# 33-point Fourier stage: a second buffer for a chunk's fp16 pair, and a chunk's loading, folding and splitting queued one unit of work sooner

## The chip, the cores and the metric

One core of a Trainium2 chip runs the whole kernel in one launch. The metric is device time in microseconds (us): the median of three runs for the kernel before, and each change is judged by its time beside it. Engines are called as in the profile: PE (TensorE, matmuls; PEld its weight loads), DVE (VectorE), ACT (ScalarE), POOL (GpSimd), SP (SyncE, which issues most DMAs).

## The reference

The input x is 4 batches of 4224 tokens with 192 features. Three layers follow each other; the change lies in the third.

```python
def _moe2_ref(x, w_ch1, w_ch2):
    X = np.fft.fft(x, axis=1)
    X = np.fft.fft(X, axis=2)
    mixed = np.real(X).astype(np.float32)
    u = x + mixed
    mu = np.mean(u, axis=-1, keepdims=True)
    var = np.mean((u - mu) ** 2, axis=-1, keepdims=True)
    un = (u - mu) / np.sqrt(var + 1e-06)
    ch = np.maximum(un @ w_ch1, 0.0) @ w_ch2
    return (u + ch).astype(np.float32)
```

The layers ahead of it are a causal softmax convolution of 7 taps, and a token mixing of rank 32 with a feed-forward net of the same shape (192 to 768 to 192, ReLU between).

## The kernel before

**Blocks.** The two feed-forward nets are the bulk of the work. 4 batches x 11 blocks of 384 tokens x 2 nets make 88 blocks, in the order net 1 of batch 0, 1, 2, then net 2 of batch 0, net 1 of batch 3, then net 2 of batch 1, 2, 3. Matmuls are made of fp16 pairs (a high part and a remainder), three or so matmuls for one. `layer1` (L623 to L629) makes two of six hidden tiles at a time: PE writes a PSUM tile, ACT takes the ReLU and its high part (`hh`, L628), DVE the remainder (`hl`, L629). `layer2` (L648 to L655) of the block before makes one of three output tiles. All PSUM tiles come from one pool of 8 buffers, and most of them are given back by a DVE instruction.

**Slots.** The program is written out by hand in slots, three to a block (r = 0, 1, 2). A slot issues two units of `layer1`, then parts of the preparation of a later block, one unit of `layer2`, and last, in `fill`, units of other work. In net 2 the preparation (`pre2`) takes statistics on DVE in slot 0 (L568 to L572), a root on ACT and the scale and shift on DVE in slot 1 (L583 to L591), and in slot 2 the normalised rows on ACT (L597, L600) and their fp16 remainder (L604, on POOL or DVE), which SP transposes into `ch`. Each engine runs its instructions in the order in which they are written here.

**The Fourier transform.** `fft_units(b)` cuts the transform of batch b in units. `fill` spreads them evenly over a window of slots (slot 0 is the first of the program): slots 37 to 69 for batch 0, 98 to 126 for batch 1, 150 to 176 for batch 2 and 190 to 214 for batch 3, so a batch has 33, 29, 27 and 25 slots for the same 17 units of its first half. The first half is the 33-point stage over 22 groups of rows, in 6 chunks of 4 (the last has 2). For one chunk c:

- `loadx(c)`: three DMAs on SP bring rows into `x33` (one buffer), and up to four gathers on POOL (L707, one each group) bring the mirrored rows into `xm` (two buffers). The first half of the gathers is called G0 here, the second G1 (the last chunk has a single gather and no G1).
- `fold(c)`: three DVE instructions (L741, L742, L744) and one of POOL (L746) add and subtract the two.
- `split33(c)`: ACT scales `xm` (L753) and writes its high part into the pair `xp` (L754), POOL its remainder (L755). `xp` has one buffer.
- `s33(c, 0)` and `s33(c, 1)`: 12 matmuls each on the pair (L774), then ACT (L781) and DVE (L782) write the result z and give the PSUM tile back.

In the list of units, the unit called a(c) holds `s33(c, 0)` and the unit m(c) holds `s33(c, 1)`. Ahead of its matmuls a(c) has `fold(c + 1)` and behind them G0 of chunk c + 2; m(c) has `split33(c + 1)` ahead and G1 of chunk c + 2 behind. Five units stand ahead of a(0); a(c) is unit 5 + 2c of 17 counted from 0, m(c) unit 6 + 2c. In batch 3 this puts every a(c) in a slot r = 2 and every m(c) in a slot r = 0, so a(c) to m(c) is one slot and m(c) to a(c + 1) two. In batch 2 the same holds from m(0) to a(3); in batches 0 and 1 the units fall on changing slots.

Of the kernel before, what the change touches and what calls it, by code (L numbers as in the profile page):

```python
# [7 lines left out]
F16 = mybir.dt.float16  # L8
# [8 lines left out]
B, S, D = 4, 4224, 192  # L17
# [18 lines left out]
XG = 4  # L36
# [59 lines left out]
def build(tc, io):  # L96
# [4 lines left out]
    def pool(name, bufs, **kw):  # L101
        return ctx.enter_context(tc.tile_pool(name=name, bufs=bufs, **kw))

    cst = pool("cst", 1)
    wrk = pool("wrk", 2)
# [10 lines left out]
    def all_max(out, x):  # L116

        ps = psm("am")
        nc.tensor.matmul(ps[:, :P], lhsT=x.broadcast_to([P, P]), rhs=sel[:, 1], start=True, stop=True)
        nc.vector.tensor_reduce(out=out, in_=ps[:, :P], axis=AX.X, op=ALU.max)  # L120

    def run(units):
        for f in units:
            if f is not None:
                f()

    with tc.manual_schedule():
# [548 lines left out]
        def fft_units(b):  # L676
# [6 lines left out]
            def scale():  # L683

                m = xmax[b]
                nc.vector.tensor_reduce(out=m[:, 11:12], in_=m[:, 0:NB], axis=AX.X, op=ALU.max)

            def scale2():
                m = xmax[b]
                all_max(m[:, 12:13], m[:, 11:12])  # L690
                nc.vector.tensor_scalar(out=m[:, 12:13], in0=m[:, 12:13], scalar1=1e-30,
                                        scalar2=2.0 ** -13, op0=ALU.max, op1=ALU.mult)
                nc.vector.reciprocal(m[:, 13:14], m[:, 12:13])
                nc.vector.tensor_scalar(out=m[:, 14:15], in0=m[:, 12:13], scalar1=2.0 ** 11,
                                        scalar2=None, op0=ALU.mult)
                st["s"], st["r"] = m[:, 13:14], m[:, 14:15]

            def loadx(c, part=None):

                g0, ng = chunks[c]  # L700
                nn = min(ng, GT - g0)
                if part != 1:
                    xs[c] = load_rows(g0, ng, nn)
                half = (nn + 1) // 2
                for g in range(nn) if part is None else (range(half), range(half, nn))[part]:
                    k = 16 + g0 + g
                    nc.gpsimd.indirect_dma_start(  # L707
                        out=xs[c][1][:, g], out_offset=None, in_=x2d[b][:],
                        in_offset=bass.IndirectOffsetOnAxis(ap=mrow[:99, k:k + 1], axis=0))

            def load_rows(g0, ng, nn):
                x = wrk.tile([99, XG, D], F32, name="x33", bufs=1)
                y = wrk.tile([99, XG, D], F32, name="xm", bufs=2)
                src = x2d[b]
                if nn < ng:
                    nc.gpsimd.memset(x[64:99, nn], 0.0)
                    nc.gpsimd.memset(y[:, nn], 0.0)
                    for i in range(2):
                        nc.sync.dma_start(
                            x[33 * i:33 * i + 33, nn],  # L720
                            bass.AP(tensor=src.tensor, offset=src.offset + 33 * 64 * i * D,
                                    ap=[[P * D, 33], [1, D]]))
                for i in range(3):
                    nc.sync.dma_start(
                        x[33 * i:33 * i + 33, :nn],
                        bass.AP(tensor=src.tensor,
                                offset=src.offset + (33 + 99 * g0 + 33 * i) * D,
                                ap=[[P * D, 33], [99 * D, nn], [1, D]]))
                return x, y

            def fold(c):

                ng = chunks[c][1]
                x, y = [t[:, :ng] for t in xs[c]]
                l, r = slice(1, 96), slice(96, 191)
                v = y[:, :, r]
                a = list(list(w) for w in v.ap)
                swap = bass.AP(tensor=v.tensor, offset=v.offset,
                               ap=[a[0], [D, ng], [-95, 2], [1, 95]])
                m = x[:, :, 1:191].rearrange("p g (h n) -> p g h n", h=2)  # L740
                nc.vector.tensor_tensor(out=m, in0=m, in1=swap, op=ALU.add)  # L741
                nc.vector.tensor_tensor(out=y[:, :, 0:97:96], in0=x[:, :, 0:192:191],  # L742
                                        in1=y[:, :, 0:192:191], op=ALU.add)
                nc.vector.tensor_tensor(out=y[:, :, l], in0=x[:, :, l], in1=x[:, :, r],  # L744
                                        op=ALU.add)
                nc.gpsimd.tensor_tensor(out=y[:, :, 97:192], in0=x[:, :, l], in1=x[:, :, r],  # L746
                                        op=ALU.subtract)

            def split33(c):
                n = chunks[c][1] * D  # L750
                x = xs[c][1].rearrange("p g d -> p (g d)")[:, :n]
                t = wrk.tile([99, 2, XG * D], F16, name="xp", bufs=1)
                nc.scalar.activation(x, x, AF.Identity, scale=st["s"][:99])  # L753
                nc.scalar.activation(t[:, 0, :n], x, AF.Identity)  # L754
                nc.gpsimd.tensor_tensor(out=t[:, 1, :n], in0=x, in1=t[:, 0, :n], op=ALU.subtract)  # L755
                xs[c] = t

            def s33(c, e):

                if "z" not in st:  # L760
                    st["z"] = z_tile().rearrange("p (e l k n) -> p e l k n", e=2, l=2, k=17)
                g0, ng = chunks[c]
                m, c0 = ((KD, 0), (D - KD, KD))[e]
                x = xs[c]
                nn = min(ng, GT - g0)
                ps = psm("s33")
                for g in range(ng):
                    if g < nn:
                        w, kr, o = tabs["w33"], 99, ps[:m, 102 * g:102 * g + 102]
                    else:  # L770
                        w, kr, o = tabs["w33s"][:, e], 66, ps[:m, 102 * g:102 * g + 34]
                    cols = slice(g * D + c0, g * D + c0 + m)
                    for n, (xq, wq) in enumerate(((0, 0), (0, 1), (1, 0))):
                        nc.tensor.matmul(o, lhsT=x[:kr, xq, cols], rhs=w[:kr, wq],  # L774
                                         start=(n == 0), stop=(n == 2))
                for a, n, o in ((1 + 3 * g0, 3 * nn, 0), (0, ng - nn, 102 * nn)):
                    if n:
                        v = ps[:m, o:o + 34 * n].rearrange("p (n k) -> p k n", k=34)
                        hi, lo = [st["z"][:m, e, l].rearrange("p k (f n) -> p (k f) n", f=2)
                                  [:, :, a:a + n] for l in range(2)]  # L780
                        nc.scalar.activation(hi, v, AF.Identity, scale=2.0 ** -11)  # L781
                        nc.vector.scalar_tensor_tensor(out=lo, in0=v, scalar=2.0 ** -11, in1=hi,  # L782
                                                       op0=ALU.mult, op1=ALU.subtract)
# [80 lines left out]
                nc.gpsimd.tensor_tensor(out=y1, in0=y1, in1=near(1, 1), op=ALU.add)  # L864

            last = len(chunks) - 1
            first = [lambda: (scale(), loadx(0)), scale2, lambda: (fold(0), loadx(1)), lambda: split33(0), None]
            for c in range(len(chunks)):
                a, m = [lambda c=c: s33(c, 0)], [lambda c=c: s33(c, 1)]
                if c < last:  # L870
                    a.insert(0, lambda c=c: fold(c + 1))
                    m.insert(0, lambda c=c: split33(c + 1))
                if c + 1 < last:
                    a.append(lambda c=c: loadx(c + 2, 0))
                    m.append(lambda c=c: loadx(c + 2, 1))
                first += [lambda a=a: run(a), lambda m=m: run(m)]
            todo = [8] + list(range(8))
            out = [lambda: (loadu(8), loadu(0)), lambda: sd(8)]
            for i, j in enumerate(todo):
                a, m = [lambda j=j: s128(j)], [lambda j=j: adds(j)]  # L880
# [106 lines left out]
        play(0)  # L987

        ft = [fft_units(b) for b in range(B)]

        windows = [[28, 32, [load_tables]],
# [16 lines left out]
        last, pre = None, [(None, None)] * 4  # L1008
        for i in range(nblk + 1):
# [15 lines left out]
            last = layer2(*blocks[i]) if i < nblk else None  # L1025
# [57 lines left out]
```

## Time and profile before

| | |
|---|---|
| median of 3 runs | 1019.2 us (1017.62 to 1020.02) |
| the profiled execution | 1028.63 us, span 1026.8 us |
| granted TensorE clock, mean | 0.997 |
| busy: PE / DVE / ACT / POOL | 989.8 / 764.0 / 605.2 / 373.9 us |
| share of the span: PE / DVE / ACT / POOL | 96% / 74% / 59% / 36% |

The profiled execution is one run of the program, and it took 9.4 us longer than the median. The span is from its first to its last instruction. Idle time of an engine is put down to what ended it: "<-POOL xp L755" is the wait that the POOL instruction of line 755 ended. A clock of 1.00 is TensorE's 2.4 GHz, 0.50 its 1.2 GHz.

### The profile page before, as it was taken

The page shows a single profiled execution, that of the slowest core. Times are in us where ns is not written, and L with a number is a line of the kernel's source. Part 1 is how long each engine was busy: PE and PEld are TensorE (multiplying, and loading weights), DVE is VectorE, ACT ScalarE, POOL GpSimd, SP SyncE. Part 2 cuts the span into 40 slices and gives each one's busy share as a digit, 9 for nine tenths or more (in the row PEclk, how much of TensorE's full clock was granted, in tenths as well). Part 3 has the DMA queues.
Part 4 walks back from the last instruction along what each step waited for, and adds up shares of the span by engine and source line. Part 5 has one row for each costly group of instructions (what it writes and reads, how often), then busy time and mean ns, then how long its engine had stood idle before and what let it go on. Part 6 is the DMA issues. An engine that isn't in the chain of part 4 may idle for free.

```text
span 1026.8 us, 25594 instructions
## 1 busy us (share of the span) xinstructions
PE 989.8 (96%) x9929; PEld 776.4 (76%) x9929; DVE 764.0 (74%) x2092; ACT 605.2 (59%) x1482; POOL 373.9 (36%) x367
## 2 busy tenths in 40 slices
PE   8789999999999999999999999999999999999998
PEld 5466777777777877777778877777887777787777
DVE  7766776788876666877777777897887687687674
ACT  2555557666766666656656666656556565555552
POOL 0001001344632333346534435663255751562100
PEclk9999999999999999999999999999999999999999
DMA  8597757665646665444344455332544342433221
GB/s 286 162 227 251 208 135 200 194 168 135 168 105 179 187 180 143 94 107 112 96 127 112 138 136 148 101 88 64 119 112 93 106 86 64 131 101 71 59 59 58
DMA packets 179283, 136.32 MB, mean 133 GB/s; under 512 B 116666, under 2 KB 152737, under 8 KB 178393
## 3 DMA queue, kind: packets, MB, share of 16 engines
q1 hardware_dynamic: 171575, 121.64, 44.5%
q0 software_dynamic: 7104, 12.70, 4.6%
q8 instruction: 77, 1.26, 0.5%
q14 instruction: 45, 0.37, 0.1%
q10 hardware_dynamic: 482, 0.35, 0.1%
HBM read 61.69 MB, written 46.11 MB: 105 GB/s over the span
## 4 chain that ended last, share of the span: by engine, by line
PE 56%; DVE 7%; issue 4%; POOL 4%; DMA 3%; ACT 0%; DVEq 0%; POOLq 0%; ACTq 0%
PE l L652 8%; PE l L648 8%; PE l L650 8%; PE l L623 5%; PE l L627 5%; PE l L624 5%; PE l L626 5%; PE l L625 5%; POOL xm L707 2%; DVE hl L629 2%; PE sd L814 2%; DMA xm<-x2d,mrow 2%; DMA ch<-sp 2%; PE s L830 2%; DVE x L741 1%
## 5 line engine op out<-in xcount | busy, mean ns | idle before, releaser
L648 PE MATMUL l<-w2h,hh 128*128 128x192 f16 x1584 | 391.0, 247 | 1.9 <-DVE u L655 0.9
L650 PE MATMUL l<-w2l,hh 128*128 128x192 f16 x1584 | 390.8, 247 | 1.5 <-DVE w2l L262 1.2
L652 PE MATMUL l<-w2h,hl 128*128 128x192 f16 x1584 | 390.8, 247 | 1.4 <-DVE hl L629 0.9
L628 ACT ACTIVATE hh<-l 128x384 f16<-128x384 f32 x528 | 249.7, 488 | 224.8 <-PE l L627 209.4
L629 DVE SCALAR_TENSOR_TENSOR hl<-l,hh 128x384 f16<-128x384 f32 x528 | 278.7, 551 | 80.4 <-ACT hh L628 72.1
L623 PE MATMUL l<-ch,w1h 128*128 128x384 f16 x528 | 172.9, 327 | 15.2 <-DMA ch<-sp 8.8
L624 PE MATMUL l<-ch,w1l 128*128 128x384 f16 x528 | 172.0, 326 | 0.7 <-issue 0.7
L627 PE MATMUL l<-ch,w1h 128*128 128x384 f16 x528 | 172.5, 327 | 0.0
L626 PE MATMUL l<-ch,w1l 128*128 128x384 f16 x528 | 172.4, 327 | 0.0
L625 PE MATMUL l<-ch,w1h 128*128 128x384 f16 x528 | 172.1, 326 | 0.0
L648 PEld LDWEIGHTS <-hh 128*128 128x128 f16 x1584 | 155.5, 98 | 19.3 <-issue 3.2
L650 PEld LDWEIGHTS <-hh 128*128 128x128 f16 x1584 | 155.5, 98 | 17.9 <-issue 2.3
L548 POOL TENSOR_TENSOR sp<-un,sp 128x576 f16<-128x576 f32 x44 | 57.3, 1301 | 300.5 <-ACT sp L544 252.5
L652 PEld LDWEIGHTS <-hl 128*128 128x128 f16 x1584 | 155.5, 98 | 4.3 <-issue 2.5
L604 POOL TENSOR_TENSOR sp<-un,sp 128x576 f16<-128x576 f32 x34 | 45.5, 1339 | 158.5 <-ACT sp L600 150.7
L707 POOL DMA_INDIRECT xm<-x2d,mrow x84 | 84.4, 1005 | 21.2 <-issue 18.0
L655 DVE SCALAR_TENSOR_TENSOR u<-l,cmax,u 128x192 f32<-128x192 f32 x132 | 54.8, 416 | 41.5 <-PE l L652 25.6
L655 DVE SCALAR_TENSOR_TENSOR u<-l,ws,u 128x192 f32<-128x192 f32 x132 | 54.4, 412 | 36.4 <-PE l L652 26.9
L623 PEld LDWEIGHTS <-w1h 128*128 128x128 f16 x528 | 51.6, 98 | 35.5 <-DMA ch<-sp 10.8
L625 PEld LDWEIGHTS <-w1h 128*128 128x128 f16 x528 | 51.5, 97 | 34.9 <-issue 0.7
L627 PEld LDWEIGHTS <-w1h 128*128 128x128 f16 x528 | 51.6, 98 | 34.3 <-issue 0.2
L626 PEld LDWEIGHTS <-w1l 128*128 128x128 f16 x528 | 51.5, 98 | 34.4 <-issue 0.2
(138 smaller groups left out, 1414.7 us busy)
## 6 DMA issues: line engine op xcount, KB each, us to landing
x2d<-u SPq DMA_DIRECT2D x68, 288.0 KB
u<-x1d SPq DMA_DIRECT2D x44, 288.0 KB
out_d<-u SPq DMA_DIRECT2D x43, 288.0 KB
x1d<-xw SPq DMA_DIRECT2D x36, 210.0 KB
u<-x2d SPq DMA_DIRECT2D x32, 192.0 KB
x<-x2d SPq DMA_DIRECT2D x60, 99.0 KB
xw<-x_d SPq DMA_DIRECT2D x4, 1344.0 KB
xw<-x_d SPq DMA_DIRECT2D x8, 672.0 KB
```

Source lines behind the costliest of these rows:

```text
L623: nc.tensor.matmul(o, lhsT=w["h1"][:, 0, ms], rhs=kd[0], start=True, stop=False)
L624: nc.tensor.matmul(o, lhsT=w["l1"][:, 0, ms], rhs=kd[0], start=False, stop=False)
L625: nc.tensor.matmul(o, lhsT=w["h1"][:, 1, ms], rhs=kd[1], start=False, stop=False)
L626: nc.tensor.matmul(o, lhsT=w["l1"][:, 1, ms], rhs=kd[1], start=False, stop=False)
L627: nc.tensor.matmul(o, lhsT=w["h1"][:, 2, ms], rhs=kd[2], start=False, stop=True)
L628: nc.scalar.activation(hh[:, m], ps[:, :TB * P], AF.Relu)
L629: nc.vector.scalar_tensor_tensor(out=hl[:, m], in0=ps[:, :TB * P], scalar=0.0, in1=hh[:, m], op0=ALU.max, op1=ALU.subtract)
L648: nc.tensor.matmul(o, lhsT=hh[:, m, rs], rhs=w["h2"][:, m], start=(m == 0), stop=False)
L650: nc.tensor.matmul(o, lhsT=hh[:, m, rs], rhs=w["l2"][:, m], start=False, stop=False)
L652: nc.tensor.matmul(o, lhsT=hl[:, m, rs], rhs=w["h2"][:, m], start=False, stop=(m == NM - 1))
L655: nc.vector.scalar_tensor_tensor(out=u[:, r], in0=o, scalar=sc, in1=u[:, r], op0=ALU.mult, op1=ALU.add)
L707: nc.gpsimd.indirect_dma_start(out=xs[c][1][:, g], out_offset=None, in_=x2d[b][:], in_offset=bass.IndirectOffsetOnAxis(ap=mrow[:99, k:k + ...
```

## The change

`xp` gets two buffers. `loadx` of the first chunks is cut into its halves, and every step of a chunk's preparation stands one unit sooner: a(c) now has `split33(c + 1)` ahead of its matmuls and G1 of chunk c + 2 behind them; m(c) has `fold(c + 2)` ahead and G0 of chunk c + 3, with its three SP loads, behind. The five units ahead of a(0) take up what moved. Lines up to L866 keep their numbers, later ones move by up to four.

```diff
-                t = wrk.tile([99, 2, XG * D], F16, name="xp", bufs=1)
+                t = wrk.tile([99, 2, XG * D], F16, name="xp", bufs=2)
...
-            first = [lambda: (scale(), loadx(0)), scale2, lambda: (fold(0), loadx(1)), lambda: split33(0), None]
+
+            first = [lambda: (scale(), loadx(0, 0)), lambda: (scale2(), loadx(0, 1)),
+                     lambda: (fold(0), loadx(1, 0)), lambda: (split33(0), loadx(1, 1)),
+                     lambda: (fold(1), loadx(2, 0))]
             for c in range(len(chunks)):
                 a, m = [lambda c=c: s33(c, 0)], [lambda c=c: s33(c, 1)]
                 if c < last:
-                    a.insert(0, lambda c=c: fold(c + 1))
-                    m.insert(0, lambda c=c: split33(c + 1))
+                    a.insert(0, lambda c=c: split33(c + 1))
                 if c + 1 < last:
-                    a.append(lambda c=c: loadx(c + 2, 0))
-                    m.append(lambda c=c: loadx(c + 2, 1))
+                    a.append(lambda c=c: loadx(c + 2, 1))
+                    m.insert(0, lambda c=c: fold(c + 2))
+                if c + 2 < last:
+                    m.append(lambda c=c: loadx(c + 3, 0))
```

The order of PE's instructions stays the same, all 17593 of them. On the other engines the steps move past their neighbours. Three places in batch 3 show it; numbers behind a name are those of a buffer or a tensor and differ between the two programs.

DVE, before: scale and shift of a block in slot 1 (L583 to L591), `layer1` and `layer2` of slot 2, then a fold at its end, and the z of `s33(c, 0)`.

```order
L583 RECIPROCAL rs<-sd 128x3
L584 TENSOR_TENSOR sd<-rs 128x3
L585 SCALAR_TENSOR_TENSOR sd<-sd,va 128x3
L587 SCALAR_TENSOR_TENSOR rs<-sd,rs 128x3
L591 SCALAR_TENSOR_TENSOR mr<-mv,rs 128x3
L629 SCALAR_TENSOR_TENSOR hl<-l_12733,hh 128x384
L629 SCALAR_TENSOR_TENSOR hl<-l_12741,hh 128x384
L655 SCALAR_TENSOR_TENSOR u_11258<-l_12755,ws_3647,u_11258 128x192
L741 TENSOR_TENSOR x_12612<-x_12612,xm 99x4x190
L742 TENSOR_TENSOR xm<-x_12612,xm 99x8
L744 TENSOR_TENSOR xm<-x_12612 99x4x95
L782 SCALAR_TENSOR_TENSOR z<-s_12783,z 97x34x12
```

DVE, now: the fold stands at the end of slot 0, and the scale and shift of slot 1 come behind it.

```order
L741 TENSOR_TENSOR x_12506<-x_12506,xm 99x4x190
L742 TENSOR_TENSOR xm<-x_12506,xm 99x8
L744 TENSOR_TENSOR xm<-x_12506 99x4x95
L782 SCALAR_TENSOR_TENSOR z<-s_12677,z 95x34x12
L629 SCALAR_TENSOR_TENSOR hl<-l_12699,hh 128x384
L629 SCALAR_TENSOR_TENSOR hl<-l_12707,hh 128x384
L655 SCALAR_TENSOR_TENSOR u_11258<-l_12717,ws_3658,u_11258 128x192
L583 RECIPROCAL rs<-sd 128x3
L584 TENSOR_TENSOR sd<-rs 128x3
L585 SCALAR_TENSOR_TENSOR sd<-sd,va 128x3
L587 SCALAR_TENSOR_TENSOR rs<-sd,rs 128x3
L591 SCALAR_TENSOR_TENSOR mr<-mv,rs 128x3
```

The fold moved from the end of slot 2 to the end of slot 0, ahead of the five instructions that make `mr` and `rs`.

ACT, before: the normalised rows of slot 2 (L597, L600), the z of `s33(c, 0)`, two ReLUs of the next slot, and then the split (L753, L754).

```order
L597 ACTIVATE un<-u_11258,mr,rs 128x192 x3
L600 ACTIVATE sp<-un 128x3x192
L781 ACTIVATE z<-s_12597 97x34x12
L628 ACTIVATE hh<-l_12621 128x384
L628 ACTIVATE hh<-l_12629 128x384
L753 ACTIVATE xm<-xm,xmax 99x768
L754 ACTIVATE xp<-xm 99x768
L781 ACTIVATE z<-s_12671 95x34x12
```

ACT, now: the split stands in slot 2, right behind the normalised rows.

```order
L597 ACTIVATE un<-u_11258,mr,rs 128x192 x3
L600 ACTIVATE sp<-un 128x3x192
L753 ACTIVATE xm<-xm,xmax 99x768
L754 ACTIVATE xp<-xm 99x768
L781 ACTIVATE z<-s_12608 97x34x12
L628 ACTIVATE hh<-l_12627 128x384
L628 ACTIVATE hh<-l_12635 128x384
L781 ACTIVATE z<-s_12677 95x34x12
```

L753 and L754 moved ahead of one z and two ReLUs, and wait with the instructions that need `mr` and `rs`.

POOL, before: from one split (L755) to the next, with G1, a block's remainder (L604), the fold's POOL part and G0 between.

```order
L755 TENSOR_TENSOR xp<-xm,xp 99x768
L707 DMA xm<-x2d_73,mrow 99x192 x2
L604 TENSOR_TENSOR sp<-un,sp 128x3x192
L746 TENSOR_TENSOR xm<-x_12426 99x4x95
L707 DMA xm<-x2d_73,mrow 99x192 x2
L755 TENSOR_TENSOR xp<-xm,xp 99x768
```

POOL, now:

```order
L755 TENSOR_TENSOR xp<-xm,xp 99x768
L707 DMA xm<-x2d_73,mrow 99x192 x2
L746 TENSOR_TENSOR xm<-x_12314 99x4x95
L707 DMA xm<-x2d_73,mrow 99x192 x2
L604 TENSOR_TENSOR sp<-un,sp 128x3x192
L755 TENSOR_TENSOR xp<-xm,xp 99x768
```

The cycle of split, G1, fold and G0 is the same; L604 moved from ahead of the fold to ahead of the next split.

## Rows read from the trace of the kernel before

**Rows 1.** Page, part 1: busy time, share of the span, instructions.

```profile
PE 989.8 (96%) x9929; PEld 776.4 (76%) x9929; DVE 764.0 (74%) x2092; ACT 605.2 (59%) x1482; POOL 373.9 (36%) x367
```

**Rows 2.** Waits of PE: who was waited for, us in total, times, longest.

```profile
PE s L774 <- POOL xp L755: 5.8, 6, 1.4
PE s L774 <- ACT xp L754: 1.2, 1, 1.2
```

**Rows 3.** Timeline of PE, batches 1 and 2: start, duration, what, [idle before, its end].

```profile
486.47 0.34 PE L623 MATMUL l<-ch,w1h 128*128 128x384 f16 x1 [0.57 <-DVE hl L629]
497.66 0.67 PE L774 MATMUL s<-vt,xp 99*97 99x102 f16 x10 [0.76 <-POOL xp L755]
511.92 0.26 PE L652 MATMUL l<-w2h,hl 128*128 128x192 f16 x1 [0.93 <-DVE hl L629]
...
681.13 0.67 PE L774 MATMUL s<-vt,xp 99*97 99x102 f16 x10 [1.16 <-POOL xp L755]
693.27 0.29 PE L774 MATMUL s<-vt,xp 99*97 99x102 f16 x2 [1.17 <-ACT xp L754]
694.99 0.67 PE L774 MATMUL s<-vt,xp 99*97 99x102 f16 x10 [1.43 <-POOL xp L755]
```

**Rows 4.** Stretches of 1 us, PE alone: length, busy, granted clock, DMA share, GB/s.

```profile
696.00:697.00 1.00, 1.00 (x5) 0.52 0.53 202
...
699.00:700.00 1.00, 1.00 (x12) 0.78 1.07 204
```

**Rows 5.** Timeline of PE, batch 3.

```profile
793.25 0.72 PE L774 MATMUL s<-vt,xp 99*97 99x102 f16 x12
...
803.69 0.72 PE L774 MATMUL s<-vt,xp 99*97 99x102 f16 x12
...
811.74 0.32 PE L623 MATMUL l<-ch,w1h 128*128 128x384 f16 x1 [0.55 <-DVE z L782]
...
819.88 0.71 PE L774 MATMUL s<-vt,xp 99*95 99x102 f16 x12
...
827.81 0.67 PE L774 MATMUL s<-vt,xp 99*97 99x102 f16 x10 [0.90 <-POOL xp L755]
...
838.90 0.67 PE L774 MATMUL s<-vt,xp 99*97 99x102 f16 x10 [0.45 <-POOL xp L755]
```

**Rows 6.** Timelines of POOL, DVE and ACT, batch 3: one round, split to split.

```profile
809.56 0.95 DVE L741 TENSOR_TENSOR x<-x,xm 99x760 f32<-99x760 f32 x1 [4.50 <-issue]
814.55 1.65 POOL L755 TENSOR_TENSOR xp<-xm,xp 99x768 f16<-99x768 f32 x1
...
817.70 1.00 POOL L707 DMA_INDIRECT xm<-x2d,mrow  x1 [0.30 <-issue]
...
821.11 0.95 DVE L741 TENSOR_TENSOR x<-x,xm 99x760 f32<-99x760 f32 x1 [2.69 <-DMA xm<-x2d,mrow]
822.35 1.24 POOL L746 TENSOR_TENSOR xm<-x 99x380 f32<-99x380 f32 x1 [1.65 <-DVE xm L742]
823.62 0.94 ACT L753 ACTIVATE xm<-xm,xmax 99x768 f32<-99x768 f32 x1 [3.12 <-POOL xm L746]
...
826.10 1.65 POOL L755 TENSOR_TENSOR xp<-xm,xp 99x768 f16<-99x768 f32 x1
```

**Rows 7.** Timelines of DVE and ACT, batch 3, first chunk: fold to split.

```profile
780.23 0.94 DVE L741 TENSOR_TENSOR x<-x,xm 99x760 f32<-99x760 f32 x1
...
784.00 1.42 ACT L597 ACTIVATE un<-u,mr,rs 128x192 f32<-128x192 f32 x3 [1.39 <-DVE rs L587]
...
786.04 0.92 ACT L753 ACTIVATE xm<-xm,xmax 99x768 f32<-99x768 f32 x1
787.00 0.84 ACT L754 ACTIVATE xp<-xm 99x768 f16<-99x768 f32 x1
```

**Rows 8.** Timeline of DVE, batch 1: folds of chunks 3 and 4.

```profile
488.35 1.83 DVE L741 TENSOR_TENSOR x<-x,xm 99x760 f32<-99x760 f32 x1 [1.11 <-DMA xm<-x2d,mrow]
502.17 0.95 DVE L741 TENSOR_TENSOR x<-x,xm 99x760 f32<-99x760 f32 x1 [3.29 <-DMA xm<-x2d,mrow]
```

## The prediction

> **What bounds the kernel now.** The page comes first: PE is busy for 989.8 of 1026.8 us, so 37 us are idle at all [rows 1], and a change off PE can give back no more than its share of them. The waits of PE say which share is this stage's: the matmuls of `s33` waited 7.0 us in seven places for the pair, 5.8 for its remainder on POOL and 1.2 for its high part on ACT [rows 2]. The timeline of PE says where: none in batch 0, 0.76 in batch 1, 1.16 + 1.17 + 1.43 in batch 2 [rows 3], and 1.16 + 0.90 + 0.45 in batch 3, of which two rows stand in [rows 5]. Behind two of them in batch 2 the granted clock drops to 1.2 GHz for a while: 0.52 at 696 us, 0.50 in the two stretches between, 0.78 at 699 [rows 4], which costs 0.48 + 0.50 + 0.50 + 0.22 = 1.7 us of PE's work.
>
> Why is the pair late? In batch 3 PE needs 803.69 - 793.25 = 10.44 us for a chunk where nothing stops it [rows 5]. The pair's own preparation takes longer. It is a round through three engines, and since POOL works in order, each chunk starts where the last one ended: split on POOL (L755) 814.55, 1.65 long; then G1, whose second gather ends at 818.70; its data land and DVE folds at 821.11, 2.41 later; POOL's part 822.35 to 823.59; ACT's L753 at 823.62 (it had waited 3.12); next split at 826.10 [rows 6]. That is 11.55 us, 1.1 more than PE's 10.44, and the waits of batch 3 are what is left of it once the head start is used up. The one buffer of the pair is not in this round.
>
> **The change, part by part.**
>
> *Second buffer.* It frees ACT's L754 from waiting for `s33(c, 1)` and removes no instruction. PE gains by it only where the split comes sooner too.
>
> *Split one unit sooner.* `s33(c + 1, 0)` now stands two units behind its split. All seven waits should go, and the drop of the clock with them: 0.76 in batch 1, 3.76 + 1.7 in batch 2, the rest in batch 3.
>
> *Fold one unit sooner.* Here is the cost. G1 and the fold that needs it were m(c) and a(c + 1), two slots apart in batch 3; they are now a(c) and m(c), one slot apart. And the fold now stands at the end of slot 0, ahead of the five DVE instructions that make `mr` and `rs`; ACT's normalised rows wait for these, and the split stands behind those rows. So the round gets another member: fold, `layer1`, `layer2` and scale and shift of the next slot on DVE, normalised rows and split on ACT, split on POOL, G1, landing, next fold. Before, the fold stood behind the scale and shift, and ACT went from the fold's POOL part straight to the split.
>
> The new round can be measured, since the first chunk of batch 3 has this order already: its fold starts at 780.23, ACT's rows at 784.00 (having waited 1.39 for DVE's `rs`), L753 at 786.04, L754 ends at 787.84 [rows 7]. That is 7.6 us. With 1.65 for the split, 2.5 to the end of G1 and 2.4 to the landing [rows 6], the round is 14.2 us. The upper end is 14.9: other chunks have a z (L782) between, and the POOL gap may add a little. The lower end is the 11.55 of before. I take 14.2, since it consists of the very instructions. A second witness: in batch 1, where fold and split were already two slots apart, two folds stand 502.17 - 488.35 = 13.8 us apart, and DVE waited 3.29 for the gathers [rows 8].
>
> The Trainium skill ("DMA: Bandwidth & Descriptors", Anatomy of one DMA) gives a gather issued from POOL a fixed 2.0 us and its bytes at 436 GB/s, about 2.2 us for 76 KB as an estimate. From the gather's issue to the fold the rows show 3.4 (1.00 and 2.41), so the trace disagrees; by the page each round would be 1.2 us shorter and the whole sum about +3 in place of +10.
>
> What does a late fold do to PE? PE can run ahead until the eight PSUM tiles are used up. Behind the last `s33` ahead of a fold there are six tiles of two slots and one more `s33`; the next needs the z that DVE writes behind the fold. The rows show this limit once: the fold of 809.56 held z, and PE waited at 811.74, 2.18 later; the `s33` ahead had ended at 804.41, and the 6.78 us of work between were done at 811.19, where the wait of 0.55 began [rows 5, 6]. So a fold may start 6.78 - 2.18 = 4.6 us behind the end of the `s33` in its unit; what is beyond that, PE waits.
>
> Batch 3: with only G0 of chunk 1 ahead of it, the first split starts as L754 ends, 787.9, and ends at 789.5; G1 to 792.0, landing and fold of chunk 1 at 794.4. Three rounds of 14.2 on, the fold of chunk 4 starts at 837.0. Its unit m(2) cannot end before 837.0 - 4.6 = 832.4; it ended at 819.88 + 0.71 = 820.6 [rows 5]. That is +11.8, less the 0.90 and 0.45 that came later and go: **+10.5**. Bounds by the two rounds: +2.5 (11.55) and +12.5 (14.9). Chunk 5 has no G1 and ends the chain.
>
> Batch 2: two such rounds (chunks 2 to 4) against 10.44 each lose 7.5; a fold that is on time stands 1.4 to 4 us behind its `s33`, so some of the 4.6 is left. I take 6.5 lost (between 2.9, all of it left, and 7.5), less 3.76 + 1.7 gained: **+1.0** (-2.6 to +2.0).
>
> Batch 1: G1 and folds move from one or two slots apart to two, and splits to one or two: rounds get shorter. The 0.76 goes, and the 0.57 and 0.93 that PE waited for DVE's `hl` behind late folds [rows 3]: **-2.3** (bounds 0 and -2.3).
>
> Batch 0: its units are two slots apart before and after, and PE never waited for a pair. 0, within 1.
>
> Clock: new waits of 14.2 - 10.44 = 3.8 us, five of them, may each bring the 1.7 us of [rows 4]; within a round that PE waits out anyway they cost nothing, which leaves the last of batch 2 and of batch 3: 0 to 3.4, and I take **+1.0**.
>
> SP's loads of `x33` move too, behind a fold that they always waited for; L604 on POOL has ended before L754 has, so neither lengthens the round. PE's order is unchanged.
>
> Sum: -2.3 + 1.0 + 10.5 + 1.0 = **+10.2**. On the profiled execution (1028.6) that is 1038.8. That execution is 9.4 us above the median, so its waits are, if anything, long; on the median of 1019.2 it is **1029.4**.
>
> **The rivals.**
>
> *A: the preparation becomes early enough and stays so.* If DVE absorbs the late folds (all of them within the 4.6 us), PE loses every old wait and gets no new one: -2.3 - 5.5 - (1.16 + 0.90 + 0.45 + 0.55) = -10.9, of which transposes and PSUM may take a part: 1008 to 1013. For it: split and matmuls are three slots apart. It holds as long as folds of batch 3 stand under 11 us apart; 3.29 us of waiting in [rows 8], with one slot between, speaks against it. The Trainium skill ("Trainium Kernel Development and Optimization", Best Practices) says "Double-buffer for performance"; by that rule this is the outcome, and the trace agrees only that the one buffer delayed L754.
>
> *B: the round stays 11.55.* Then the fold of chunk 4 starts at 794.4 + 3 x 11.55 = 829.1, batch 3 loses 2.5, batch 2 loses 2.2 to two rounds and gains 5.5, batch 1 gains 2.3: -3.1, 1016. It needs ACT's rows not to wait for the fold, against the order shown.
>
> *C: an exchange.* The new waits are as long as the old: within 2 us of 1019.
>
> *D: worse than the sum.* Each new wait drops the clock, and rows and transposes fall behind as well: +16, 1035.
>
> **How the numbers follow.** The forecast has 0.58, A 0.13, B 0.08, C 0.10, D 0.11. A measurement of this kernel can tell about 0.2% (2 us) from no change, so A and B are faster (0.21), C is the same (0.10), forecast and D are slower (0.69). The predicted time is 1029.4. The forecast's own range is 1022 to 1037, from its bounds; to leave out no more than 2 in 10 the range takes in B and C below and most of D above: 1014 to 1038.
>
> **What would show it.** Right: in batch 3 folds (L741) 14 us apart with DVE idle ahead of each until the gathers land; L753 right behind L600 without waiting for POOL; PE waiting some 4 us a chunk for DVE's z or `hl`, and none for L755; from 793 to the last `s33` about 10 us more than before; batch 1 without waits of PE. Wrong: folds of batch 3 under 12 us apart, or folds more than 5 us behind their `s33` with PE still at work, or PE waits in batch 3 that sum to less than 4 us.

## The result, and the profile after

The changed kernel takes 1034.63 us (median of four runs, 1030.99 to 1038.01), the kernel before 1018.41 in the same comparison: ratio 1.0146, 95% interval 1.0118 to 1.0174. It is 16 us slower.

The busy times of all engines are nearly those of before [rows 1], part 1 of the page of the changed kernel:

```profile
PE 997.0 (96%) x9929; PEld 780.8 (75%) x9929; DVE 752.7 (73%) x2092; ACT 609.6 (59%) x1482; POOL 373.4 (36%) x367
```

PE's 7 us more go with the same number of matmuls at a lower clock (mean granted clock 0.985, before 0.997). The rest is waiting. Waits of PE in the changed kernel (who was waited for, us in total, times, longest):

```profile
PE l L623 <- DVE z L782: 12.8, 5, 3.6
PE l L623 <- DMA ch<-sp: 8.5, 9, 2.4
PE l L623 <- DVE hl L629: 3.4, 3, 1.6
PE l L652 <- DVE hl L629: 1.7, 2, 0.9
```

The 5.8 and 1.2 us for the pair [rows 2] are gone without a trace. In their place stand five waits for z, 12.8 us. Timeline of PE: two of them in batch 2, three in batch 3, and the longest wait for `ch`, in batch 0, where PE waited 1.2 us for it at most before:

```profile
288.71 0.34 PE L623 MATMUL l<-ch,w1h 128*128 128x384 f16 x1 [2.37 <-DMA ch<-sp]
...
671.53 0.32 PE L623 MATMUL l<-ch,w1h 128*128 128x384 f16 x1 [2.01 <-DVE z L782]
686.00 0.48 PE L623 MATMUL l<-ch,w1h 128*128 128x384 f16 x1 [2.20 <-DVE z L782]
...
808.53 0.32 PE L623 MATMUL l<-ch,w1h 128*128 128x384 f16 x1 [2.79 <-DVE z L782]
823.06 0.32 PE L623 MATMUL l<-ch,w1h 128*128 128x384 f16 x1 [2.24 <-DVE z L782]
837.51 0.48 PE L623 MATMUL l<-ch,w1h 128*128 128x384 f16 x1 [3.55 <-DVE z L782]
```

Batch 1 has no wait of PE left; the three of [rows 3] are gone there.

Where the five waits come from is one round of batch 3, fold to fold, put together from the timelines of DVE, ACT and POOL. It answers to [rows 6]:

```profile
806.37 0.95 DVE L741 TENSOR_TENSOR x<-x,xm 99x760 f32<-99x760 f32 x1 [2.70 <-DMA xm<-x2d,mrow]
...
807.61 1.22 POOL L746 TENSOR_TENSOR xm<-x 99x380 f32<-99x380 f32 x1 [3.14 <-DVE xm L742]
...
810.43 0.16 DVE L591 SCALAR_TENSOR_TENSOR mr<-mv,rs 128x3 f32<-128x3 f32 x1
810.69 1.42 ACT L597 ACTIVATE un<-u,mr,rs 128x192 f32<-128x192 f32 x3 [6.03 <-DVE mr L591]
...
812.74 0.92 ACT L753 ACTIVATE xm<-xm,xmax 99x768 f32<-99x768 f32 x1
812.91 1.28 POOL L604 TENSOR_TENSOR sp<-un,sp 128x576 f16<-128x576 f32 x1 [1.58 <-ACT sp L600]
...
814.66 1.65 POOL L755 TENSOR_TENSOR xp<-xm,xp 99x768 f16<-99x768 f32 x1 [0.47 <-ACT xp L754]
816.49 1.01 POOL L707 DMA_INDIRECT xm<-x2d,mrow  x1 [0.18 <-issue]
817.80 1.00 POOL L707 DMA_INDIRECT xm<-x2d,mrow  x1 [0.30 <-issue]
...
820.88 0.95 DVE L741 TENSOR_TENSOR x<-x,xm 99x760 f32<-99x760 f32 x1 [2.78 <-DMA xm<-x2d,mrow]
```

Read it as a ring. The fold holds back `mr`, ACT sat idle for 6.03 us until `mr` came, the split stands behind ACT's rows, the gathers of G1 behind the split, and the next fold behind their data. It goes round in 820.88 - 806.37 = 14.51 us; the two rounds beside it took 13.82 and 14.46. DVE idles 2.7 us a round for data that were asked for late: the gather issued at 817.80 landed 2.7 us later, at the short end of the 2.6 to 4.5 us that the profile has for this kernel's gathers.

Sums by stage follow, from the start of a batch's first `s33` to the start of its last one in PE's timeline. The first profiled execution of before had a disturbance of its own, so a second one (e7 below) stands beside it.

| us | batch 0 | batch 1 | batch 2 | batch 3 | span |
|---|---|---|---|---|---|
| before, first profile | 81.80 | 69.84 | 68.83 | 59.83 | 1026.8 |
| before, second profile | 81.81 | 70.10 | 67.58 | 56.38 | 1018.0 |
| changed kernel | 85.46 | 66.78 | 70.79 | 71.58 | 1036.2 |
| changed less second | +3.65 | -3.32 | +3.21 | +15.20 | +18.2 |

The four terms sum to 18.7 and account for the 18.2 of the spans. In batch 3 PE waits 0.2 us in all in the second profile of before and 10.4 us in the changed kernel; the rest of its +15.20 goes with a lower clock.

### The profile page after: what moved, and what is told of

Its sections match the earlier page's. It is cut to its first block, busy times and chain, and to the rows that moved or that the text cites. A ratio compares the mean times of both kernels' runs of the same rounds, so it can differ in the third digit from the quotient of the medians.

```text
span 1036.2 us, 25568 instructions
## 1 busy us (share of the span) xinstructions
PE 997.0 (96%) x9929; PEld 780.8 (75%) x9929; DVE 752.7 (73%) x2092; ACT 609.6 (59%) x1482; POOL 373.4 (36%) x367
## 3 DMA queue, kind: packets, MB, share of 16 engines
q0 software_dynamic: 7104, 12.70, 4.4%
## 5 line engine op out<-in xcount | busy, mean ns | idle before, releaser
L628 ACT ACTIVATE hh<-l 128x384 f16<-128x384 f32 x528 | 252.8, 490 | 237.3 <-PE l L627 234.7
L623 PE MATMUL l<-ch,w1h 128*128 128x384 f16 x528 | 174.1, 330 | 25.7 <-DVE z L782 12.8
L548 POOL TENSOR_TENSOR sp<-un,sp 128x576 f16<-128x576 f32 x44 | 56.5, 1283 | 308.6 <-ACT sp L544 257.4
L604 POOL TENSOR_TENSOR sp<-un,sp 128x576 f16<-128x576 f32 x34 | 44.8, 1318 | 157.7 <-ACT sp L600 148.3
L707 POOL DMA_INDIRECT xm<-x2d,mrow x84 | 85.1, 1014 | 20.5 <-issue 17.2
L597 ACT ACTIVATE un<-u,mr,rs 128x192 f32<-128x192 f32 x132 | 62.2, 536 | 44.0 <-DVE mr L591 44.0
L624 PEld LDWEIGHTS <-w1l 128*128 128x128 f16 x528 | 52.0, 98 | 37.7 <-issue 18.3
L627 PEld LDWEIGHTS <-w1h 128*128 128x128 f16 x528 | 52.1, 99 | 35.3 <-issue 1.7
L626 PEld LDWEIGHTS <-w1l 128*128 128x128 f16 x528 | 52.0, 98 | 35.2 <-issue 1.5
L625 PEld LDWEIGHTS <-w1h 128*128 128x128 f16 x528 | 51.9, 98 | 35.3 <-issue 1.4
```

What stands on the lines that cost most here:

```text
L597: nc.scalar.activation(un[:, t], u[:, t], AF.Identity, scale=k["r"][:, t:t + 1], bias=k["m"][:, t:t + 1])
L623: nc.tensor.matmul(o, lhsT=w["h1"][:, 0, ms], rhs=kd[0], start=True, stop=False)
L624: nc.tensor.matmul(o, lhsT=w["l1"][:, 0, ms], rhs=kd[0], start=False, stop=False)
L625: nc.tensor.matmul(o, lhsT=w["h1"][:, 1, ms], rhs=kd[1], start=False, stop=False)
L626: nc.tensor.matmul(o, lhsT=w["l1"][:, 1, ms], rhs=kd[1], start=False, stop=False)
L627: nc.tensor.matmul(o, lhsT=w["h1"][:, 2, ms], rhs=kd[2], start=False, stop=True)
```

## The experiments

The theory at the start: the ring above makes the loss, and nothing of it is due to the second buffer. Rivals: the buffer itself, the fold's place alone, or DVE's own load.

**e1: the buffer without the shift.** The kernel before, with one edit:

```diff
-                t = wrk.tile([99, 2, XG * D], F16, name="xp", bufs=1)
+                t = wrk.tile([99, 2, XG * D], F16, name="xp", bufs=2)
```

> The kernel before with nothing but the second buffer of the pair. Theory (the loss is the fold's new place and the long round it makes; the buffer is harmless): folds of batch 3 stay 11 to 12 us apart, PE still waits for the pair in batches 2 and 3 (together 4 to 7 us), the time is within 3 us of before, about 1017. Rival (the buffer itself costs, for instance because another tile moves or ACT then runs ahead and delays the ReLUs): 1025 or more.

Measured: 1017.02 us, ratio 0.9968 (0.9953 to 0.9983). Its stages take 81.84, 69.33, 67.43 and 56.03 us. The waits for the pair stay, 3.6 and 1.2:

```profile
PE s L774 <- POOL xp L755: 3.6, 4, 1.4
PE s L774 <- ACT xp L754: 1.2, 1, 1.2
```

The second profile of before has 3.5 and 1.2. So the buffer does not remove these waits, as the prediction had it. What it removes are ACT's waits of L754 for `s33`, 2.0 us in three places before and none in e1. Of the 3 us that e1 is faster, the profiles show 1.2 in the four stages; where the rest lies is open. All of the loss belongs to the shift.

**e2: G1 taken out of the ring.** The changed kernel, with G1 ahead of the split:

```diff
-                    a.append(lambda c=c: loadx(c + 2, 1))
+                    a.insert(0, lambda c=c: loadx(c + 2, 1))
```

(the first list of units likewise.)

> The changed kernel, but in a(c) the second half of the gathers (G1) stands ahead of the split instead of behind it. On POOL the gathers of the next chunk then no longer follow the split, so the round fold, scale and shift, normalised rows, split, G1, fold is cut. Theory: folds of batch 3 are 10.4 to 11.5 us apart with no idle DVE ahead of them, PE waits neither for the pair nor for z: before less its old waits, 1006 to 1013. Rival 1 (what hurts is that G1 and the fold are one slot apart): G1 is still one slot ahead of the fold, DVE keeps waiting 2 to 3 us a chunk and the time stays above 1028. Rival 2 (the fold's place on DVE alone hurts, since it delays scale and shift by its own 1.6 us): about 1025.

Measured: 1026.98 us, ratio 1.0086 (1.0060 to 1.0113), folds 12.4 us apart. Against the 1.0146 of the change that is a gain of some 6 us, and well short of the 1006 to 1013 that was expected; the time is nearer to that of rival 2. POOL's timeline in e2 says what had not been thought of:

```profile
815.66 1.01 POOL L707 DMA_INDIRECT xm<-x2d,mrow  x1 [0.19 <-POOL xm L746]
816.98 1.00 POOL L707 DMA_INDIRECT xm<-x2d,mrow  x1 [0.30 <-issue]
819.56 1.27 POOL L604 TENSOR_TENSOR sp<-un,sp 128x576 f16<-128x576 f32 x1 [1.58 <-ACT sp L600]
821.02 1.01 POOL L707 DMA_INDIRECT xm<-x2d,mrow  x1 [0.19 <-issue]
822.34 1.00 POOL L707 DMA_INDIRECT xm<-x2d,mrow  x1 [0.30 <-issue]
823.36 1.66 POOL L755 TENSOR_TENSOR xp<-xm,xp 99x768 f16<-99x768 f32 x1
```

G1 no longer waits for the split, but it stands behind L604, which waits for ACT's rows (1.58 idle), which wait for `mr`. The ring closed again through POOL.

**e3: the fold behind the scale and shift.** The changed kernel, batch 3 one slot later, so that its folds fall at the end of slot 1:

```diff
-                   [190, 215, ft[3][0]], [219, 237, ft[3][1]]]
+                   [191, 216, ft[3][0]], [219, 237, ft[3][1]]]
```

> The changed kernel with the window of batch 3 one slot later (191 to 215 in place of 190 to 214), so folds stand at the end of slot 1, behind scale and shift, and splits in slot 0, behind the next two ReLUs and not right behind the normalised rows. G1 and fold are still one slot apart, fold and split two. Theory (the member 'scale and shift, normalised rows' makes the round long): folds of batch 3 come 11 to 12 us apart in place of 13.8 to 14.5, and the time falls by 6 to 9 us, to 1026 to 1029. Rival (the distance of one slot between G1 and fold does it): folds stay 14 us apart, 1032 to 1036.

Measured: 1029.62 us, ratio 1.0091 (1.0069 to 1.0113); batch 3 takes 61.96 us instead of 71.58, its rounds 12.3 to 12.5, a little over the 11 to 12 expected, and by the ratios the gain is 5.6 us, just under the 6 to 9. The fold now stands behind `mr` and no longer holds it back: with that, 2 us go out of each round. (All units of the batch moved by a slot, so this is not that link alone.) The fold holds other work up instead. Waits of PE in e3, where `hl` takes the place of z in batch 3 (the two for z lie in batch 2):

```profile
PE l L652 <- DVE hl L629: 7.2, 5, 2.8
PE l L623 <- DVE z L782: 5.7, 2, 3.6
```

**e4: G1 ahead of the split in the kernel before.**

```diff
-                    m.append(lambda c=c: loadx(c + 2, 1))
+                    m.insert(0, lambda c=c: loadx(c + 2, 1))
```

> The kernel before with one buffer and its old places, but with G1 ahead of the split in m(c). This cuts the round of 11.55 us of before. Theory (the waits of before come from the round through POOL, not from the one buffer): PE's waits for the pair in batch 3 (2.5 us) go and those of batch 2 shrink, 1011 to 1016. Rival (the one buffer makes the pair late): the waits for the pair stay at 5 us or more and the time stays within 2 us of before.

Measured: 1019.29 us, ratio 0.9997 (0.9986 to 1.0008): no change, a miss. DVE no longer waits for gathers in batch 3 and the folds still stand 12.06 us apart. POOL in e4:

```profile
801.02 1.01 POOL L707 DMA_INDIRECT xm<-x2d,mrow  x1 [0.18 <-POOL xm L746]
...
804.93 0.99 POOL L707 DMA_INDIRECT xm<-x2d,mrow  x1 [0.30 <-issue]
805.95 1.66 POOL L755 TENSOR_TENSOR xp<-xm,xp 99x768 f16<-99x768 f32 x1
```

Four gathers in a row take 5 us of POOL's queue, and the split, whose input had been ready since L754 ended at 802.68, starts at 805.95. What the fold gained, the split lost: PE's waits for the pair are 6.8 us.

**e5: a chunk loaded whole, right behind the fold.** The changed kernel with all four gathers in m(c), ahead of L604 and of the split:

```diff
-                    a.append(lambda c=c: loadx(c + 2, 1))
...
-                    m.append(lambda c=c: loadx(c + 3, 0))
+                    m.append(lambda c=c: loadx(c + 3))
```

(the first list of units likewise.)

> The changed kernel, but a chunk's rows, its sums' first operand and all four gathers are queued together right behind the fold that frees them, ahead of POOL's remainder L604 and of the split L755. Theory (the round fold, L746, gathers, landing, next fold sets the pace of the last stage, and what stands on POOL between the halves makes it long): from a fold's start 1.2 to L746, 1.2 for it, 0.2, four gathers 5.3, 2.4 to land: 10.3 us a round instead of 14.5, so PE's own work (about 11 us) decides; folds of the last 33-point stage 10.5 to 11.5 us apart, no wait of PE for z or the pair over 0.6 us, 1008 to 1014. Rival (POOL's four gathers only push L604 and L755 back by 2.6 us, and the block's transposed tile ch or the pair is late instead): PE waits of 1 to 2.5 us for ch or xp in each round, 1016 to 1024.

Measured: 1024.01 us, ratio 1.0037 (1.0019 to 1.0055): a miss for the theory, at the upper end of the rival. The rounds are 11.9 us, shorter than the 14.5 of the change, but not the 10.5 to 11.5 expected. Batch 3 takes 59.20 us, 12.4 less than in the changed kernel, but e1's 56.03 it does not reach, and batch 0 takes 89.48 with two waits for `ch` of 2.8 us. In batch 3 the gathers are out of the ring: the fold follows L572 without waiting for data. Timelines of DVE and ACT in e5:

```profile
812.40 0.95 DVE L741 TENSOR_TENSOR x<-x,xm 99x760 f32<-99x760 f32 x1 [0.20 <-issue]
...
816.48 0.16 DVE L591 SCALAR_TENSOR_TENSOR mr<-mv,rs 128x3 f32<-128x3 f32 x1
816.74 1.42 ACT L597 ACTIVATE un<-u,mr,rs 128x192 f32<-128x192 f32 x3 [3.54 <-DVE mr L591]
...
819.73 0.84 ACT L754 ACTIVATE xp<-xm 99x768 f16<-99x768 f32 x1
820.48 0.50 ACT L781 ACTIVATE z<-s 97x408 f16<-97x408 f32 x1
821.02 0.59 DVE L782 SCALAR_TENSOR_TENSOR z<-s,z 97x408 f16<-97x408 f32 x1 [3.12 <-ACT z L781]
...
824.26 0.95 DVE L741 TENSOR_TENSOR x<-x,xm 99x760 f32<-99x760 f32 x1 [0.20 <-issue]
```

There is a second ring, with no gather in it: fold, `mr`, ACT's rows, split, and the z (L781) that stands behind the split on ACT; DVE waits 3.12 for that z, and the next fold stands behind it. It takes 11.86 us, 1.4 more than PE's 10.44. This ring is read from the rows; no kernel here broke it by itself.

**e6 and e8: L604 off POOL.** The kernels of e2 and e5, with one edit each (`LOWV` lists the blocks whose remainder is made on DVE):

```diff
-        LOWV = [[59, 67], [72, 74]]
+        LOWV = [[59, 74]]
```

> The kernel of e2_g1_ahead, with the remainder L604 of all blocks of the last 33-point stage on DVE instead of POOL. Theory: in e2 the second half of the gathers stood behind L604, which waits for ACT's normalised rows, and that alone made its rounds 12.4 us; with L604 gone from POOL the four gathers stand together behind L746, and the round is that of e5: folds 10.5 to 11.5 us apart in the last stage, 1010 to 1018 (DVE has 5 remainders more there, each longer than on POOL's queue would matter). Rival (the round is set by DVE's own queue, the scale and shift ahead of the fold): folds stay 12 to 13 us apart, 1024 to 1030.

> e5_load_whole with the remainder L604 of the last 33-point stage on DVE. If e5 shows waits for ch behind a late L604, they go here, and the time is 1 to 8 us below e5; if e5 has none, the time is that of e5 or up to 5 us above, by DVE's added work.

Measured: e6 1027.14 us, ratio 1.0065 (1.0040 to 1.0089), against e2's 1.0086 (1.0060 to 1.0113); folds of batch 3 11.9 to 12.3 us apart. That is a miss for the theory: taking L604 out of POOL's queue gives 0.3 us a round, not the 1 to 2 expected, and the intervals of the two times overlap. It fits a second ring of 11.9 right behind the first. e8: 1.0049 (1.0031 to 1.0068), not to be told from e5, so in e5 L604 on POOL cost nothing that shows.

**e7: the kernel before, once more.**

> The kernel before, unchanged, for a second profile: if the first profiled execution (1028.6) held some 9 us that are not the kernel's, this one lies at 1017 to 1021, the idle pieces between the stages that nothing in the records ended are gone, and the waits for the pair in the last 33-point stage stay (5.8 + 1.2 us, rounds of about 11.6 us).

Measured, in one run: 1019.8 us, span 1018.0. The wait of 4.50 us ahead of the fold in [rows 6], which the records put down to nothing, is not there. Waits of DVE put down to nothing, for that line: the first profile of before, then the second.

```profile
DVE x L741 <- issue: 4.9, 3, 4.5
```

```profile
DVE x L741 <- issue: 0.5, 3, 0.2
```

Batch 3 is 3.45 us shorter without it (56.38), so the profile on which the prediction was built had a batch 3 that was too long. The waits for the pair are 3.5 and 1.2 here, not 5.8 and 1.2, and none of them lies in batch 3: its folds stand 11.6 to 12.0 us apart, and PE goes through its chunks in 10.44 us all the same. That they would stay there is a miss; e1 shows none there either (0.2 us).

**e9 to e12: one batch at a time.** Two buffers everywhere; the order of the change in the named batch alone, in the others the order of before:

```diff
+            if b in (1,):
...
+            else:
+                first = [lambda: (scale(), loadx(0)), scale2, lambda: (fold(0), loadx(1)), lambda: split33(0), None]
```

e10 has (3,) there, e11 and e12 (0,); e12 has also `LOWV = [[11, 24], [59, 67], [72, 74]]`, which puts the remainder L548 of the blocks beside batch 0 on DVE.

> Two buffers for the pair everywhere; the shifted units in batch 1's 33-point stage alone, the order of before in the other three. Theory (each batch's stage stands for itself): batch 1's stage from its first to its last 33-point transform takes 66.8 us as in the changed kernel, against 69.3 in e1_buffer_only; the others keep e1's 81.8, 67.4 and 56.0; 1017.0 - 2.5 = 1014.5, between 1012.5 and 1016, faster than both kernels. Rival (what a stage gains is given back in the next, where the same engines wait): batch 1 at 66.8, but the time of e1_buffer_only, 1016 to 1018.

> The shifted units in batch 3 alone, with two buffers. Theory: batch 3 holds nearly all of the loss by itself, its rounds 14.2 to 14.5 us against 12.0 in e1_buffer_only, the stage 71 to 72 us against 56.0: 1017.0 + 15 = 1032, between 1029 and 1034. Rival (the rounds are long because the batches before have already put the queues late): 58 to 65 us in that stage, 1019 to 1026.

> The shifted units in batch 0 alone, with two buffers. Theory: the 3.7 us that the prediction had at zero belong to batch 0's shift: its stage 85 to 86 us against 81.8, with one wait of PE for ch of 2 to 3 us near 288 and half clock behind it: 1017.0 + 3.6 = 1020.6, between 1019 and 1022. Rival (scatter of one profiled execution): 81 to 83 us, 1016 to 1018.

> e11_shift_b0 with the remainder L548 of the ordinary blocks beside that stage on DVE, behind the block's adds, instead of on POOL behind L746, the memsets and a gather. Theory (ch is late since L548 stands on POOL behind a L746 that waits for the late fold): the wait for ch near 288 goes to under 0.8 us, the stage to 82 to 83.5 us, 1017 to 1019. Rival (DVE itself, held 2.2 us by the fold, makes the adds and all behind them late): the wait and the stage stay within 1 us of e11_shift_b0, the time within 1 us or above it.

In this comparison the kernel before took 1032.35 us in 23 runs (1029.54 to 1034.05), so only ratios and stages are compared with the others.

| kernel | us | ratio (95%) | b0 | b1 | b2 | b3 |
|---|---|---|---|---|---|---|
| e9, batch 1 | 1026.93 | 0.9953 (0.9936 to 0.9969) | 81.82 | 68.23 | 67.66 | 59.81 |
| e10, batch 3 | 1040.68 | 1.0079 (1.0062 to 1.0096) | 81.83 | 69.98 | 69.01 | 70.77 |
| e11, batch 0 | 1032.73 | 1.0006 (0.9992 to 1.0020) | 84.38 | 69.95 | 67.13 | 59.88 |
| e12, batch 0, L548 on DVE | 1033.23 | 1.0019 (1.0003 to 1.0035) | 85.79 | 69.95 | 67.26 | 59.79 |

e10: batch 3 makes its loss by itself, 70.77 us, with rounds of 13.87, 14.54 and 14.40; no earlier batch is needed for it. The ratio is lower than the 1.0117 that 1032 stood for. That fits batch 3 of the other orders, which takes 59.8 and not 56.0 here: the wait of 4.5 us put down to nothing is there again (4.47 in e9, 4.85 in e11, 4.72 in e12). The kernel before has no profile from this comparison.

e11: batch 0 loses by its own shift, 84.38 against 81.8, and by the ratios (1.0006 against e1's 0.9968) some 4 us; it is no scatter. The 85.46 of the changed kernel hold half clock as well, which e11 does not show behind its wait of 2.35 us at the same place. e9 beats the kernel before, and the changed one; whether it beats e1 (0.9968, 0.9953 to 0.9983) the intervals leave open, and its batch 1 takes 68.23, not the 66.8 expected.

e12 is a miss: its stage is 1.4 us longer than e11's. Its wait for `ch` near 289 shrank from 2.35 to 1.27, and the one near 241 grew from 1.47 to 3.08, with a clock of 0.50 for 3 us behind it that e11 does not have there. Timeline of SP's queue and of PE, e11 first, then e12:

```profile
236.93 1.31 SPq L557 DMA_TRANSPOSE ch<-sp  x1
...
240.97 0.34 PE L623 MATMUL l<-ch,w1h 128*128 128x384 f16 x1 [1.47 <-DMA ch<-sp]
```

```profile
233.20 1.64 SPq L557 DMA_TRANSPOSE ch<-sp  x1
...
241.09 0.50 PE L623 MATMUL l<-ch,w1h 128*128 128x384 f16 x1 [3.08 <-DMA ch<-sp]
```

With L548 on DVE the transposing DMA was issued 3.7 us sooner, and the tile came no sooner. So POOL's queue is not what makes `ch` late near 241. In e12 that DMA ran beside the rows of `x33` and the next block's rows; whether they held it up was not tried.

## Why the prediction was right, and where its terms were off

It said slower, 1029.4 in a range of 1014 to 1038; measured were 1034.6. Step by step:

- *The round.* Foretold were 14.2 us through fold, scale and shift, rows, split, G1 and landing; measured 13.8 to 14.5. The member taken from [rows 7], fold to the end of L754, was 7.6 there and is 814.53 - 806.37 = 8.16 in the ring above. e2 (gathers out) and e3 (scale and shift out) each bear out a link of it, and e10 that no other batch is needed.
- *The limit of 4.6 us* from the end of an `s33` to the fold in its unit. The folds at 806.37, 820.88 and 835.34 started 7.42, 6.85 and 8.44 us behind the `s33` of their units (which ended at 798.95, 814.03 and 826.90). Less 4.6 that makes waits of 2.8, 2.25 and 3.8; PE waited 2.79, 2.24 and 3.55. Only the place was off: m(2) was not held to 832.4, its matmuls ended at 826.90 and PE waited behind them.
- *Batch 3, +10.5*: right against the profile that it was read from (59.83 to 71.58, +11.75), 5 too small against an undisturbed one (+15.2). The step that failed is taking "820.6" as the undisturbed end of m(2). It was 27.3 us behind the first `s33`, and is 25.3 in the second profile; the 4.50 us of DVE in [rows 6] stand ahead of it. I used this very row for the limit, and did not ask whether its wait belonged to the kernel. Nor were the 0.90 and 0.45 there to be gained: without that wait the round of 11.55 us, which I held for the cause of batch 3's waits, cost PE nothing (e7). From the second profile the same working gives 837.0 - 793.25 - 4.6 - 25.3 = +13.9.
- *Batch 2, +1.0*: +2.0 against the first profile, +3.2 against the second, where there was less to gain (67.58 instead of 68.83). The waits of 2.01 and 2.20 came where foretold, 4.2 us in all instead of 6.5. Against the second profile PE waits 0.4 us more in the whole stage; the rest of the +3.2 goes with a lower clock (below).
- *Batch 1, -2.3*: -3.1 and -3.3, beyond its bound. PE has no wait left there. e9 alone gives 68.23 instead of 69.3 to 70.1; in e2, e5, e6 and e8 the stage takes 66.77.
- *Batch 0, 0 within 1*: wrong, +3.7. The argument was that its units stand two slots apart before and after. It left out what stands behind the fold on DVE. The changed kernel's timelines of DVE, POOL and ACT, batch 0:

```profile
279.75 0.95 DVE L741 TENSOR_TENSOR x<-x,xm 99x760 f32<-99x760 f32 x1 [2.24 <-DMA xm<-x2d,mrow]
...
281.00 1.24 POOL L746 TENSOR_TENSOR xm<-x 99x380 f32<-99x380 f32 x1 [4.02 <-DVE xm L742]
...
284.02 0.36 ACT L529 ACTIVATE junk<-u 128x192 f16<-128x192 f32 x1 [2.40 <-DVE u L520]
284.10 1.29 POOL L548 TENSOR_TENSOR sp<-un,sp 128x576 f16<-128x576 f32 x1
```

  The fold waited 2.24 us for its gathers, POOL 4.02 for the fold with L548 behind it, and ACT 2.40 for DVE's adds of the next block (L520). PE waited 2.37 us for `ch` at 288.71 and then ran at half clock (0.50 from 290 to 293). In the whole stage PE waits 3.6 us for `ch` instead of 1.8, and the half clock costs 1.7. e11 shows 2.6 of the term with the shift of batch 0 alone; e12 shows that L548's place on POOL is not all of it.
- *Clock, +1.0 in the sum*: too small. The clock fell behind four of the five waits for z. Behind the first of batch 2 and the first of batch 3 (671.53, 808.53) the next wait takes up the loss, as argued. Behind the last of each (686.00, 837.51) none follows, and there the lower level costs 1.6 and 2.7 us: 4.3, where the bounds were 0 to 3.4. These are parts of the stages' terms. The clock goes with the scatter of the four runs as well: 1030.99 us at a mean clock of 0.993, 1033.54 at 0.991, 1035.73 at 0.987, 1038.01 at 0.985.
- *The medians.* The sum was made against an execution of 1028.6 and laid on the median of 1019.2 as it was, with the remark that its waits "are, if anything, long". That had the wrong sign for the sum: the execution's batch 3 was too long, so the distance to the changed kernel was too short. The forecast was 5.2 us low. Term by term it misses more: the measured stages sum to +18.7 where it had +10.2, by 3.7 in batch 0, 2.2 in batch 2 and 4.7 in batch 3 (3.5 of it the disturbance), less 1.0 in batch 1 and the 1.0 that the sum had for the clock on top. The changed kernel's profiled execution, 1038.01, is itself 3.4 above its median, so part of that is not in the medians.
- The fixed cost of a gather in the Trainium skill ("DMA: Bandwidth & Descriptors", Anatomy of one DMA) would have given +3 by the estimate of 2.2 us from issue to landing. In the changed kernel the second gather is issued at 817.80 and the fold starts at 820.88, 3.1 us later; its data landed 2.7 us behind the issue. The sum by the Trainium skill's figure would have missed by 13 us.
- The Trainium skill ("Trainium Kernel Development and Optimization", Best Practices) says "Double-buffer for performance", and it says it of overlapping DMA with compute. On this buffer, which ACT and POOL write and PE reads, it bears only by likeness. e1 agrees within its small size, -3 us, for the buffer; the sentence says nothing of the order in which the two halves are prepared, and there the 16 us were lost.

## What to carry to other kernels

A step that is queued sooner on in-order engines goes ahead of everything it is moved past. Before moving it, follow the new order once round, from the step through all engines back to the same step of the next piece, and add up the ring: if it is longer than the bottleneck's work for one piece, the move makes a new bound, however early each step looks. And before a sum is built on one profiled execution, look for idle time that nothing ended; it may come from how that execution's transfers happened to meet, and not from the kernel's order.

## What the runs showed of the hardware

**Waits that nothing ended.** In the first profile of before, and in e9, e11 and e12, DVE sat idle for 15.8, 18.4, 16.3 and 15.3 us in all without a cause in the records; in e10 it was 9.6, in the second profile of before and in e1 1.5 and 1.8. In the first four the largest piece stands at the same instruction, the fold of chunk 2 of batch 3 (4.50, 4.47, 4.85 and 4.72 us). The DMA packets show what this fold lacked. DMA queues of the kernel before from 805.6 to 808.2 us, and below from 808.4 to 808.6 (queue, kind: packets, MB, share of 16 engines):

```profile
q0 software_dynamic: 45, 0.08, 7.7%
q8 instruction: 1, 0.02, 3.5%
...
q0 software_dynamic: 3, 0.00, 0.9%
```

A gather is 48 packets of queue 0 (7104 for 148 gathers). Of the last gather ahead of this fold 45 came by 807.4 us and three only at 808.5, and the fold started 1.0 us behind them at 809.56. Beside them, from 805.96 to 807.43, one load of 16 KB of instructions ran. e9, e11 and e12 show the same, and in all four the three late packets come 1.0 to 1.1 us behind the end of the load; in the second profile of before all 48 came between 800.5 and 801.5, and the load began at 802.2. So the fold waited for its data. That the load held up the three packets is likely from this order, and no run tested it. The other pieces of idle time stay open, and so does why the kernel before took 1029.5 to 1034.1 us in all 23 runs of the last comparison and about 1020 in the two before.

**The clock behind a wait.** PE alone in stretches of 1 us, changed kernel (length, busy, granted clock, DMA share, GB/s):

```profile
808.00:809.00 1.00, 0.47 (x3) 0.87 0.00 0
809.00:810.00 1.00, 1.00 (x5) 0.50 0.11 22
...
811.00:812.00 1.00, 1.00 (x6) 0.50 0.45 128
...
823.00:824.00 1.00, 0.94 (x6) 1.00 0.00 0
...
838.00:839.00 1.00, 1.00 (x4) 0.50 0.07 22
...
842.00:843.00 1.00, 1.00 (x9) 0.57 0.50 194
```

Behind the wait of 2.79 us (PE back at 808.53) the engine ran at 1.2 GHz for three stretches, and behind the wait of 2.24 (back at 823.06) at 2.4 GHz throughout. But 2.20 us at 686.00 did bring the lower level: 0.50 over the 3 us from 686. So the length of the wait alone does not decide it. In the wait of 3.55 us the clock fell before PE was back at 837.51, and it stayed at 0.50 until 842.
